# An attention and MLP kernel on one core: 25 words of its hand-written order of steps change places

## The chip, the core and the metric

The kernel runs on one core of a Trainium2 chip. The metric is device time in microseconds (us) of one execution, median over runs. The core has five engines with instruction queues of their own: PE (TensorE, the matmuls), DVE (VectorE), ACT (ScalarE), POOL (GpSimd) and SP (SyncE, which here only issues DMAs). DMAs issued by SP go through one queue (q1 in the profile, "hardware dynamic"), those issued by POOL through another (q0, "software dynamic"). Both queues are served by the same 16 DMA engines.

## The reference

```python
scores = scale * q @ k.T                      # 8 batches x 8 heads, 576 positions, 64 wide
cum = cumsum(maximum(s, 0))
bias = -(cum[:, None] - cum[None, :])
scores = where(causal, -1e9, scores + minimum(bias, 0))
attn = softmax(scores)
x = concat_heads(attn @ v)                    # 8 x 576 x 512
xn = (x - mean(x)) / sqrt(var(x) + 1e-6) * g_ln
out = x + relu(xn @ w_ch1) @ w_ch2            # 512 -> 2048 -> 512
```

## The kernel before

The work is one list of steps, `PLAN` (from L1318), written out by hand. A loop at its end calls each word's function in that order; every function issues instructions to one or more engines, and each engine then runs its own instructions strictly in that order. Nothing reorders them later, so an instruction that waits holds back all that stands behind it on its engine, and a DMA that waits on SP holds back every later DMA of SP.

There are three phases. Batch 0 is done tile by tile (128 positions at a time, tile 4 being the last 64): `T.t.g` transposes, `S.t.g.i` scores, `x` exponentials, `V.t.g` times v, `N` normalises, `B`, `A` and `L.t` take the LayerNorm statistics and apply them, `X.t` transposes the result for the MLP. Batch 1 goes head by head: `s.n` scores of head n (8 to 15), `d.n` the scores of its last 64 positions, `v.n` times v, `n.n` normalisation. Batches 2 to 7 go by pairs of heads: `B2.n` the scores of pair n, `bx` exponentials (ACT), `bm` causal masks (POOL), `Y.n.i` times v (PE), `K.n.i` normalisation (DVE). The MLP of each batch is cut into units that the words `u` and `U` take one by one from a queue and that fill PE between the attention steps: 512-wide matmuls of the first product (`ph`, L792) and of the second (`py`, L811); in batch 0 part of the first product is cut by tiles (`piece`, L1087).

Data come in two ways:

- POOL's queue, float32 to bfloat16 on the way: `w1.c` and `w2.i` are quarters of the two MLP weights (512 KB of bfloat16 each, L253 and L256), `lp.g` is `kp` and `qp` of pair g (L184; pairs 4 to 7 are batch 1's, 8 to 11 batch 2's), `LV.b.t` a tile of v (L192). POOL gives its DMAs eight completion semaphores in turn, so a DMA is issued only when the one eight places ahead of it has landed.
- SP's queue, float32: `lr.b.t` loads one tile of k and one of q of batch b (L206, `rowtmp`, 256 KB each), `lv.b.t` one tile of v. POOL casts k and q (`cr`, L218) and weights v (`vm`, L233); `tr` transposes by DMA (L225). `aug` (the words `aug` and `a3`, L265 and L267) copies rows of the gate sums beside q and k; `a3` writes into `kq[1]`, which batch 0's scores of heads 4 to 7 read, so it waits for the last of these.

`Q.q.g` and `Q.k.g` are the transposes of pair g on PE (`trqk`, L323), which read `qp` and `kp`; `E` copies them out of PSUM. `W.n` is n dummy matmuls (`idle`, L889). `Sk` are the scores of batch 0's last 64 keys (L1014). `fv.0` clears a part of `v_bf` (POOL). `Da.b.4` is a DMA transpose on SP (L759), `la.b.t` LayerNorm of tile t of batch b (DVE).

Of the kernel before, what the change touches and what calls it, by code (L numbers as in the profile page):

```python
# [16 lines left out]
P = 128  # L17
# [13 lines left out]
def fast_path(  # L31
# [13 lines left out]
    B, H, S, D = q.shape  # L45
# [13 lines left out]
    G = 4  # L59
# [896 lines left out]
    E = {"A": "act", "D": "dve", "P": "pool", "S": "sync"}  # L956
# [249 lines left out]
    def raise_flag(count, ones, n):  # L1206
# [120 lines left out]
        S.3.0.2 B.0.1 T.3.1 B.1.0 x.2.1.0 e.3.1:D B.1.1 S.3.0.0 S.3.0.3 y.0:A aug x.3.0.2 V.2.0 M.0.0.0 x.3.0.3
        M.0.0.3 S.3.0.1 V.2.1 S.3.1.1 x.3.0.1 N.2.0 M.0.0.2 bc.4 S.3.1.3 x.3.0.0 X.1 x.3.1.3 y.1:A N.2.1 M.0.0.1
        S.3.1.2 V.3.0 S.3.1.0 M.0.1.3 L.2 T.4.0 M.0.1.0 r.0.0:A N.3.0 X.2 x.3.1.2 Q.q.4 x.3.1.0 x.3.1.1 e.4.0:D
        T.4.1 y.2:D M.0.1.2 Q.k.4 E.q.4.0:A B.3.0 E.k.4.0:A S.4.0.1 e.4.1:D S.4.1.0 M.0.1.1 E.q.4.1:D E.k.4.1:D  # L1330
        x.4.0.1 x.4.1.0 U A.1 V.3.1 s.8 N.3.1 u L.3 B.2.1 B.2.0 d.8 S.4.0.0 X.3 y.3:A r.0.1:D Q.q.5 E.q.5.1:A
# [287 lines left out]
```

## Time and profile before

| | us |
|---|---|
| median of 3 runs | 344.21 (342.92 to 344.62) |
| the profiled execution | 346.36 |
| its span, first to last instruction | 344.9 |
| PE busy in the span | 331.5 |
| DVE, ACT, POOL busy | 199.5, 187.7, 168.6 |

The profiled execution is 2.15 us (0.6%) above the median of the runs; its span is 1.46 us shorter than its time. Times of the views are microseconds from the start of the span. A timeline row gives start, duration, engine, line, operation, output and input, count, and in brackets how long the engine sat idle before it and what released it. A windows row gives the window and its length, then busy time and instructions of PE, PEld, DVE, ACT and POOL, the clock granted to PE as a share, the mean busy share of the DMA engines (over 1 where packets overlap), and GB/s.

### The profile page before, as it was taken

The page shows a single profiled execution, that of the slowest core. Times are in us where ns is not written, and L with a number is a line of the kernel's source. Part 1 is how long each engine was busy: PE and PEld are TensorE (multiplying, and loading weights), DVE is VectorE, ACT ScalarE, POOL GpSimd, SP SyncE. Part 2 cuts the span into 40 slices and gives each one's busy share as a digit, 9 for nine tenths or more (in the row PEclk, how much of TensorE's full clock was granted, in tenths as well). Part 3 has the DMA queues.
Part 4 walks back from the last instruction along what each step waited for, and adds up shares of the span by engine and source line. Part 5 has one row for each costly group of instructions (what it writes and reads, how often), then busy time and mean ns, then how long its engine had stood idle before and what let it go on. Part 6 is the DMA issues. An engine that isn't in the chain of part 4 may idle for free.

```text
span 344.9 us, 8061 instructions
## 1 busy us (share of the span) xinstructions
PE 331.5 (96%) x3117; PEld 183.3 (53%) x3117; DVE 199.5 (58%) x567; ACT 187.7 (54%) x348; POOL 168.6 (49%) x305
## 2 busy tenths in 40 slices
PE   6999989989998998999999999999999999999993
PEld 2899756545554554555555545554455444444443
DVE  6598777837685675347653664566448624523421
ACT  4998899677664675357736774486344204202200
POOL 8896768777377947683984377441301001000000
PEclk9899999999999999999999999999999999999998
DMA  9999999999999999999998966700510141020022
GB/s 144 181 189 177 172 193 195 214 208 233 164 215 227 169 245 195 216 228 198 205 209 205 214 108 151 139 2 2 121 63 2 24 129 46 3 90 33 2 62 65
DMA packets 147962, 48.59 MB, mean 141 GB/s; under 512 B 135280, under 2 KB 143760, under 8 KB 147920
## 3 DMA queue, kind: packets, MB, share of 16 engines
q1 hardware_dynamic: 121856, 38.34, 57.3%
q0 software_dynamic: 24304, 8.92, 22.0%
q10 hardware_dynamic: 1760, 0.79, 0.9%
q8 instruction: 25, 0.41, 0.5%
q14 instruction: 17, 0.14, 0.1%
HBM read 37.11 MB, written 9.44 MB: 135 GB/s over the span
## 4 chain that ended last, share of the span: by engine, by line
PE 77%; DMA 10%; POOL 7%; DVE 1%; issue 1%; SPq 1%; ACT 0%; POOLq 0%; DVEq 0%
PE py L811 34%; PE ph L792 31%; DMA v_bf<-in_v_dram 5%; PE pot L626 4%; DMA kp<-in_k_dram 3%; PE sa L553 2%; DMA rowtmp<-in_k_dram 2%; PE sb L553 1%; PE sc L553 1%; PE pott L664 1%; DMA rowtmp<-in_v_dram 1%; POOL rowb L180 1%; PE pot L590 1%; SPq L206 1%; POOL v_bf L233 1%
## 5 line engine op out<-in xcount | busy, mean ns | idle before, releaser
L811 PE MATMUL py<-w_bf,hT 128*128 128x512 bf16 (+2 forms) x608 | 131.1, 368 | 0.1
L792 PE MATMUL ph<-xT,w_bf 128*128 128x512 bf16 x480 | 109.8, 379 | 0.2 <-ACT er L560 0.2
L783 ACT ACTIVATE hT<-ph 128x512 bf16<-128x512 f32 x102 | 60.9, 604 | 77.6 <-PE ph L792 76.1
L811 PEld LDWEIGHTS <-hT 128*128 128x128 bf16 x608 | 55.9, 98 | 59.8
L792 PEld LDWEIGHTS <-w_bf 128*128 128x128 bf16 x544 | 51.3, 98 | 56.5 <-issue 0.3
L497 POOL TENSOR_SCALAR_AFFINE_SELECT er<-er 128x256 bf16<-128x256 bf16 x96 | 38.8, 419 | 48.7 <-ACT er L560 34.3
L823 DVE SCALAR_TENSOR_TENSOR yo<-py,rstd,xb 128x512 f32<-128x512 f32 x32 | 24.0, 751 | 50.5 <-PE py L811 46.2
L560 ACT ACTIVATE er<-sb 128x512 bf16<-128x512 f32 x48 | 28.2, 609 | 22.1 <-PE sb L553 17.9
L781 DVE TENSOR_SCALAR hT<-ph 128x512 bf16<-128x512 f32 x34 | 23.5, 691 | 27.5 <-PE ph L792 26.0
L233 POOL TENSOR_TENSOR v_bf<-rowtmp,wt 128x512 bf16<-128x512 f32 (+1 forms) x30 | 33.1, 1107 | 10.0 <-DMA rowtmp<-in_v_dram 9.8
L560 ACT ACTIVATE er<-sa 128x512 bf16<-128x512 f32 x48 | 28.6, 609 | 16.4 <-PE sa L553 15.1
L560 ACT ACTIVATE er<-sc 128x512 bf16<-128x512 f32 x48 | 28.8, 614 | 3.8 <-PE sc L553 3.8
L626 PEld LDWEIGHTS <-er 128*128 128x128 bf16 x480 | 19.8, 97 | 12.8 <-POOL er L497 4.0
L715 POOL TENSOR_TENSOR rstd<-rstd,mhalf 128x4 f32<-128x4 f32 (+1 forms) x8 | 8.7, 1093 | 34.3 <-DVE rstd L714 34.2
L626 PE MATMUL pot<-v_bf,er 128*128 128x66 bf16 x480 | 22.5, 193 | 3.1 <-POOL er L497 2.1
L700 DVE BATCH_NORM_STATS2 stats<-xb 128x6 f32<-128x128 f32 (+1 forms) x84 | 24.8, 326 | 0.6
L741 DVE SCALAR_TENSOR_TENSOR xn<-xb,mv,gb 128x512 bf16<-128x512 f32 x28 | 24.5, 874 | 1.0
L218 POOL CAST kq<-rowtmp 128x512 bf16<-128x512 f32 (+1 forms) x30 | 19.0, 645 | 12.2 <-DMA rowtmp<-in_k_dram 11.8
L643 DVE TENSOR_REDUCE sums<-pot 128x4 f32<-128x8 f32 x48 | 7.8, 163 | 29.5 <-PE pot L626 29.1
L645 DVE TENSOR_TENSOR xb<-pot,rinvs 128x256 f32<-128x256 f32 x48 | 20.4, 424 | 1.7
L553 PEld LDWEIGHTS <-kq 64*128 64x128 bf16 x384 | 11.9, 94 | 9.6 <-issue 4.2
L218 POOL CAST rowb<-rowtmp 128x512 bf16<-128x512 f32 (+1 forms) x20 | 12.8, 652 | 3.3 <-DMA rowtmp<-in_k_dram 2.9
(178 smaller groups left out, 393.2 us busy)
## 6 DMA issues: line engine op xcount, KB each, us to landing
out_dram<-yo SPq DMA_DIRECT2D x32, 256.0 KB
rowtmp<-in_v_dram SPq DMA_DIRECT2D x24, 256.0 KB
rowtmp<-in_k_dram SPq DMA_DIRECT2D x20, 256.0 KB
rowtmp<-in_q_dram SPq DMA_DIRECT2D x20, 256.0 KB
w_bf<-in_moe_w_ch_dram POOLq DMA_DIRECT2D x8, 512.0 KB, 9.0
kp<-in_k_dram POOLq DMA_DIRECT2D x8, 144.0 KB, 10.2
qp<-in_q_dram POOLq DMA_DIRECT2D x8, 144.0 KB, 10.2
v_bf<-in_v_dram POOLq DMA_DIRECT2D x8, 128.0 KB, 8.3
```

The lines of the kernel that those rows point to most:

```text
L218: nc.gpsimd.tensor_copy(out=rows[b % 2][0:pn, t, u], in_=loaded.pop(("kq"[u], b, t))[0:pn])
L233: e.tensor_tensor(out=v_bf[b % 2][0:pn, t, :, 0:D], in0=loaded.pop(("v", b, t))[0:pn], in1=wt[0:pn, t, b, :].unsqueeze(2).to_broadcast([pn ...
L497: nc.gpsimd.affine_select(out=out, in_=out, compare_op=ALU.is_ge, fill=0.0, base=0, pattern=pattern, channel_multiplier=-1,)
L553: nc.tensor.matmul(a, lhsT=lhsT, rhs=rhs, start=True, stop=True)
L560: nc.scalar.activation(out=er[:, 2 * n % 4 + i, o : o + 512], in_=bank["B", n].pop((name, i)), func=ACT.Exp, scale=scale,)
L626: nc.tensor.matmul(pot[:, t, :], lhsT=e[:, o : o + P], rhs=v_bf[b % 2][:, kb, h, :], start=(kb == 0), stop=(kb == t),)
L700: nc.vector.bn_stats(out=st[b][:, t, part, :], in_=x_tiles(b)[t][:, lo:hi])
L741: nc.vector.scalar_tensor_tensor(out=xn, in0=tiles[t], scalar=mvs[b][:, t, 0:1] if b > 0 else mean0[:, t : t + 1], in1=gb, op0=ALU.subtrac ...
L783: nc.scalar.activation(out=dst, in_=ph, func=ACT.Relu)
L792: nc.tensor.matmul(ph, lhsT=w1_bf[:, kd, fb * P : (fb + 1) * P], rhs=xT[:, :, kd, :], start=(kd == 0), stop=(kd == KD - 1),)
L811: nc.tensor.matmul(py[t], lhsT=hT[:, fb, t * P : (t + 1) * P], rhs=w2_bf[:, fb, c0:c1], start=(fb == 0), stop=(fb == FB - 1),)
L823: nc.vector.scalar_tensor_tensor(out=yo, in0=py[t], scalar=rs, in1=x[:, c0:c1], op0=ALU.mult, op1=ALU.add)
```

## The change

The words stay the same 1305; 25 of them stand elsewhere. The table's rows tell little, so only two lines of its diff are shown:

```diff
-        lc.k.3 lc.q.3 g LV.0.2 w1.0 LV.0.3 lp.4 cr2.0 cr2.1 fv.1 fk.0 fk.1 lc.k.4 lc.q.4 w1.1 f.7 f.8 fv.0 lp.5
-        w1.2 f.9 f.10 LV.1.0 LV.1.1 LV.1.2 LV.1.3 LV.1.4 lp.6 LV.0.4 w1.3 w2.0 lp.7 lp.8 w2.1 f.11 relu.0 scan.0
+        lc.k.3 lc.q.3 g LV.0.2 w1.0 LV.0.3 lp.4 cr2.0 cr2.1 fv.1 fk.0 fk.1 lc.k.4 lc.q.4 w1.1 f.7 f.8 w1.2 fv.0
+        lp.5 f.9 f.10 LV.1.0 LV.1.1 LV.1.2 LV.1.3 LV.1.4 lp.6 LV.0.4 w1.3 w2.0 lp.7 lp.8 w2.1 f.11 relu.0 scan.0
...
```

By words:

- `w1.2` goes ahead of `fv.0` and `lp.5`.
- `W.1` (one dummy matmul) goes from between `T.0.0` and `hi.2` to just behind `scan.0`, so that it joins the nine at the start.
- `L.1` goes behind the two steps `B.0.1` and `B.1.0`.
- Around the end of batch 0: `S.4.1.1` goes ahead of `S.4.0.0`; `Q.q.5` and `Sk` ahead of `r.0.1`; `d.8` and `Q.k.5` behind the next `u wr u`; `B.0.0` and a `U` ahead of `v.8`.
- `a3` goes from ahead of `lr.3.1` to behind `N.4.1`, so on SP `lr.3.1` now stands ahead of it.
- Later: `K.9.0` ahead of `vm.3.0` and the LayerNorm of batch 1's last tile; `Da.1.4` and `bx.16.4` some ten words later; `la.3.1`, `lv.5.4`, `cr.6.3.0`, `cr.6.4.0`, `cr.6.1.0` and `Y.20.1` later.

On SP, near its start, the two loads of `lr.3.1` (`rowtmp`, k and q) and the four copies of `a3` into `kq_110` change places:

```order
 L265 DMA kq_111<-c_122 1x4x576
 L267 DMA kq_111<-c_122 1x4x576 x3
+L206 DMA rowtmp<-in_k_dram 128x8x64
+L206 DMA rowtmp<-in_q_dram 128x8x64
 L265 DMA kq_110<-c_122 1x4x576
 L267 DMA kq_110<-c_122 1x4x576 x3
-L206 DMA rowtmp<-in_k_dram 128x8x64
-L206 DMA rowtmp<-in_q_dram 128x8x64
 L206 DMA rowtmp<-in_v_dram 128x8x64
 L206 DMA rowtmp<-in_k_dram 128x8x64
```

The two loads have moved ahead of four copies that wait for PE; the loads themselves wait only for DMAs of the first microseconds, and their staging tiles are fresh. Everything behind keeps its order.

On POOL, between its early memsets, `w1.2` (`w_bf`) and the pair `lp.5` (`kp`, `qp`) change places:

```order
 L934 MEMSET v_bf_108 128x32
 L935 MEMSET v_bf_108 64x8
+L253 DMA w_bf<-in_moe_w_ch_dram 128x4x512
 L1314 MEMSET v_bf_107 64x528
 L184 DMA kp<-in_k_dram 96x2x384
 L184 DMA qp<-in_q_dram 96x2x384
-L253 DMA w_bf<-in_moe_w_ch_dram 128x4x512
 L937 MEMSET kq_111 128x8x64
 L192 DMA v_bf_108<-in_v_dram 128x8x64 x4
```

The weight quarter is now issued one memset and two loads sooner, and `kp` and `qp` of pair 5 stand behind it in the queue.

More of the change, by code (lines that the diff above doesn't have):

```diff
@@ L1327, in fast_path @@
[L1327 to L1331, printed above, removed]
@@ L1392, in fast_path @@
[L1392 to L1396 removed]
+        S.2.1.1 N.1.1 S.2.0.0 L.0 V.1.0 x.2.0.1 x.2.0.2 x.2.1.2 X.0 e.3.0:D N.1.0 x.2.1.1 x.2.0.0 S.2.1.0
@@ new lines, in fast_path @@
+        S.3.0.2 B.0.1 T.3.1 B.1.0 x.2.1.0 L.1 e.3.1:D B.1.1 S.3.0.0 S.3.0.3 y.0:A aug x.3.0.2 V.2.0 M.0.0.0
+        x.3.0.3 M.0.0.3 S.3.0.1 V.2.1 S.3.1.1 x.3.0.1 N.2.0 M.0.0.2 bc.4 S.3.1.3 x.3.0.0 X.1 x.3.1.3 y.1:A N.2.1
+        M.0.0.1 S.3.1.2 V.3.0 S.3.1.0 M.0.1.3 L.2 T.4.0 M.0.1.0 r.0.0:A N.3.0 X.2 x.3.1.2 Q.q.4 x.3.1.0 x.3.1.1
+        e.4.0:D T.4.1 y.2:D M.0.1.2 Q.k.4 E.q.4.0:A B.3.0 E.k.4.0:A S.4.0.1 e.4.1:D S.4.1.0 M.0.1.1 E.q.4.1:D
+        E.k.4.1:D x.4.0.1 x.4.1.0 U A.1 V.3.1 s.8 N.3.1 u L.3 B.2.1 B.2.0 S.4.1.1 S.4.0.0 X.3 y.3:A Q.q.5 Sk
@@ new lines, in fast_path @@
+        r.0.1:D E.q.5.1:A E.q.5.0:D x.4.1.1 x.4.0.0 u wr u d.8 Q.k.5 u B.0.0 U v.8 La.3 E.k.5.0:D B.3.1 n.8 xk
+        cr.3.0.0 lr.3.1 Q.k.6 E.k.6.0:A E.k.5.1:A u s.9 V.4.1 E.k.6.1:D N.4.1 a3 M.0.2.3 M.0.2.2 V.4.0 Q.q.6
+        N.4.0 s.10 v.9 A.3 qu.3 M.0.2.0 lp.11 d.10 A.2 M.0.2.1 E.q.6.0:D s.11 n.9 u Q.k.7 E.q.6.1:D w2.2 d.12
+        s.12 r.0.2:A E.k.7.0:D E.k.7.1:D O2.k.8:A v.10 n.10 Q.q.7 u s.13 E.q.7.0:D w2.3 E.q.7.1:D wT v.11 lp.10
+        u wx n.11 ga.1.0.2 lv.2.0 A.0 u d.14 ga.1.0.0 v.12 qu.4 n.12 O2.k.9:A s.14 cr.3.1.0 ga.1.0.3 u F.k.8
@@ new lines, in fast_path @@
+        v.13 u R qu.5 n.13 La.6 F.k.9 ga.1.1.2 s.15 v.14 u G.k.9:D ga.1.1.0 n.14 U v.15 O2.q.8:A O2.q.9:A U n.15
+        F.q.9 qu.6 lr.3.2 O2.k.11:A vo.2:P u ga.1.2.0 ga.1.2.1 ga.1.0.1 La.2 me cr.3.1.1 u l.0 O2.q.11:A F.q.8 U
+        ga.1.1.3 ga.1.1.1 lv.2.1 l.1 lv.2.2 G.k.8:A ga.1.2.2 vm.2.0:P vo.3:P ga.1.2.3 lr.3.3 F.k.11 lv.2.3 u l.3
+        F.q.11 cr.3.0.1 lv.2.4 l.2 G.q.11:D G.q.8:A G.q.9:A cr.3.2.0 G.k.11:A O2.k.10:A D lr.3.4 u U F.k.10 U
+        O2.q.10:A G.k.10:A F.q.10 to G.q.10:A u lv.3.0 U lr.4.0 tk.2 vm.2.1:P B2.8 vm.2.2:P bx.8.3 u bx.8.1
@@ new lines, in fast_path @@
+        vm.2.3:P sd.2 bx.8.4 vm.2.4:P bx.8.2 qu.7 se.2 u bx.8.5 sm.2 ga.1.0.4 u bx.8.0 bm.8.3 u bm.8.1 B2.9
+        bm.8.2 bm.8.0 bx.9.5 Y.8.1 ga.1.1.4 lr.4.1 cr.3.2.1 bx.9.4 cr.3.3.0 bx.9.0 Y.8.0 cr.3.3.1 K.8.0 tr.3.0.2
+        bm.9.3 cr.3.4.1 K.8.1 bx.9.2 bm.9.0 bx.9.3 bx.9.1 bm.9.1 u bm.9.2 U u u Y.9.0 K.9.0 vm.3.0:P ga.1.2.4
+        la.1.4 B2.10 bx.10.0 bx.10.3 bx.10.4 bx.10.2 bx.10.5 cr.3.4.0 bm.10.3 bx.10.1 Y.9.1 U K.9.1 u tr.3.2.4 u
+        U u lv.3.1 tr.3.4.5 bm.10.1 Y.10.1 bm.10.0 B2.11 bx.11.0 bx.11.4 lv.3.2 bx.11.5 lv.3.3 K.10.1 bm.10.2
@@ new lines, in fast_path @@
+        Y.10.0 K.10.0 bm.11.2 ga.2.0.0 lv.3.4 bx.11.2 bm.11.0 La.4 bx.11.1 u ga.2.1.2 ga.2.0.3 U u cr.4.1.1
+        lr.4.2 bx.11.3 Y.11.0 K.11.0 bm.11.3 u U bm.11.1 u ga.2.0.1 lr.4.3 cr.4.0.1 vm.3.1:P Y.11.1 K.11.1
+        lv.4.0 lv.4.1 tk.3 vm.3.4:P lr.4.4 u ga.2.1.0 u Z.2 z.2 B2.12 bx.12.0 vm.3.2:P U bx.12.4 bm.12.2
+        ga.2.1.1 bx.12.1 lv.4.2 ga.2.2.0 cr.4.2.1 ga.2.2.1 ga.2.1.3 lv.4.3 la.2.0 la.2.1 cr.4.0.0 bx.12.5
+        bm.12.3 vm.3.3:P cr.4.1.0 ga.2.2.2 bx.12.3 bm.12.1 u bx.12.2 bm.12.0 u u sd.3 se.3 u B2.13 bx.13.5
@@ new lines, in fast_path @@
+        bx.13.1 ga.2.0.2 la.2.2 u bx.13.0 cr.4.4.0 sm.3 u bx.13.4 ga.2.2.3 u la.2.3 Da.2.0 bx.13.3 u Y.12.0
+        bx.13.2 bm.13.0 K.12.0 u u B2.14 cr.4.4.1 tr.4.4.5 bx.14.2 Y.12.1 K.12.1 bx.14.1 bm.13.2 bx.14.3 vo.4:P
+        bx.14.4 u u u tr.4.0.2 bx.14.5 bm.13.1 bm.13.3 bx.14.0 Y.13.0 B2.15 bx.15.0 K.13.0 bx.15.2 cr.4.3.1
+        cr.4.2.0 cr.4.3.0 tr.4.2.4 u lr.5.0 u vm.4.1:P Y.13.1 bx.15.3 bx.15.5 bx.15.1 u K.13.1 bx.15.4 bm.14.1
+        bm.14.2 bm.15.0 tk.4 ga.3.0.0 U U bm.14.0 u bm.15.1 Y.14.0 K.14.0 bm.14.3 Y.14.1 K.14.1 sd.4 ga.3.1.1
@@ new lines, in fast_path @@
+        ga.3.1.3 ga.3.1.0 se.4 u vm.4.0:P u u lv.4.4 bm.15.3 lv.5.0 Y.15.1 ga.3.0.1 K.15.1 vm.4.3:P Z.3 z.3
+        B2.16 bx.16.0 bx.16.2 vm.4.2:P bm.15.2 Y.15.0 K.15.0 sm.4 vm.4.4:P bx.16.3 bx.16.1 bm.16.1 bx.16.5
+        bm.16.3 u ga.3.2.3 U bm.16.0 lr.5.1 cr.5.1.0 ga.3.1.2 cr.5.0.0 u Da.1.4 bx.16.4 u ga.3.0.3 lv.5.2
+        ga.3.0.2 u u bm.16.2 u Y.16.0 ga.3.2.1 cr.5.1.1 ga.3.2.0 lr.5.3 cr.5.3.0 B2.17 bx.17.0 bx.17.1 la.3.0
+        vm.5.2:P K.16.0 bx.17.4 lr.5.4 lr.6.0 lv.5.3 Y.16.1 lr.5.2 K.16.1 bm.17.2 lv.5.1 ga.3.2.2 cr.5.4.0 u
@@ new lines, in fast_path @@
+        cr.5.4.1 bx.17.2 bx.17.3 bm.17.0 la.3.2 la.3.3 cr.5.2.0 bm.17.1 tr.5.4.5 bx.17.5 bm.17.3 lr.6.1 u la.3.1
+        u qm u u cr.5.3.1 u cr.5.2.1 u tk.5 vo.5:P cr.6.1.1 Da.3.0 u lv.6.0 u Y.17.0 B2.18 bx.18.3 bx.18.2
+        bx.18.0 K.17.0 bx.18.1 u u Y.17.1 K.17.1 bx.18.4 bx.18.5 bm.18.3 tr.5.2.4 u u ga.3.1.4 ga.3.0.4 B2.19
+        bx.19.0 vm.5.3:P bx.19.3 bm.18.2 ga.4.0.1 bm.18.1 cr.5.0.1 bm.18.0 tr.5.0.2 vm.5.0:P bx.19.1 u bm.19.1 u
+        u lv.6.1 sd.5 u bx.19.5 lv.5.4 se.5 Y.18.1 sm.5 K.18.1 u vm.5.1:P Y.18.0 ga.3.2.4 la.3.4 bx.19.2 U u u U
@@ new lines, in fast_path @@
+        ga.4.0.3 bm.19.3 bx.19.4 bm.19.2 u u ga.4.0.2 u K.18.0 ga.4.1.0 bm.19.0 Y.19.0 K.19.0 Z.4 z.4 B2.20
+        bx.20.0 vm.5.4:P ga.4.1.2 bx.20.2 lr.6.2 lr.6.3 Y.19.1 K.19.1 ga.4.2.2 bx.20.3 bx.20.4 bm.20.2 lv.6.2
+        bm.20.0 cr.6.2.0 ga.4.2.3 u ga.4.2.0 u vm.6.1:P bx.20.5 bm.20.3 cr.6.0.1 bx.20.1 u u u ga.4.1.1 bm.20.1
+        ga.4.0.0 Y.20.0 K.20.0 u u u u cr.6.3.1 lr.6.4 lr.7.0 lv.6.3 ga.4.2.1 vo.6:P B2.21 bx.21.4 bm.21.2
+        lr.7.1 la.4.0 la.4.1 u bx.21.1 ga.4.1.3 cr.6.3.0 cr.6.4.0 Y.20.1 K.20.1 la.4.2 bx.21.2 bx.21.0 cr.6.4.1
@@ new lines, in fast_path @@
+        bm.21.0 cr.6.1.0 cr.6.2.1 u u bx.21.3 u u tr.6.4.5 Y.21.0 bx.21.5 bm.21.3 B2.22 u bx.22.0 la.4.3 Da.4.0
+        bm.21.1 K.21.0 bx.22.4 cr.6.0.0 tr.6.0.2 bx.22.3 u u bx.22.5 bm.22.3 u Y.21.1 bx.22.2 La.7 K.21.1
+        cr.7.1.0 bx.22.1 bm.22.2 tk.6 u u vm.6.3:P tr.6.2.4 B2.23 bx.23.2 bx.23.4 bx.23.0 bx.23.3 bm.22.0
+        bm.22.1 bx.23.1 u u u vm.6.0:P bx.23.5 bm.23.0 u sd.6 se.6 u u Y.22.1 u cr.7.0.1 K.22.1 ga.5.0.0 Y.22.0
+        K.22.0 ga.5.0.1 u u bm.23.3 lr.7.2 u vm.6.2:P cr.7.1.1 bm.23.1 Y.23.1 K.23.1 bm.23.2 Z.5 z.5 B2.24
@@ new lines, in fast_path @@
+        bx.24.0 Y.23.0 ga.5.0.3 K.23.0 lr.7.3 lv.6.4 bx.24.3 ga.5.1.4 ga.5.2.4 cr.7.3.0 lv.7.0 sm.6 ga.5.1.3
+        bx.24.4 bm.24.2 ga.5.2.0 u lv.7.1 La.5 ga.5.2.1 u u bx.24.2 bm.24.0 ga.5.1.1 U vm.6.4:P ga.5.1.0 la.5.0
+        bx.24.5 bx.24.1 bm.24.3 vm.7.0:P ga.5.0.4 lv.7.2 u bm.24.1 lv.7.3 ga.5.2.2 u u Y.24.0 K.24.0 Da.3.4 u u
+        lr.7.4 cr.7.4.0 u ga.5.2.3 u cr.7.0.0 tr.7.0.2 cr.7.4.1 tr.7.4.5 lv.7.4 B2.25 bx.25.2 bx.25.4 vo.7:P
+        bx.25.0 bx.25.5 bx.25.1 bx.25.3 bm.25.2 la.5.1 Y.24.1 u K.24.1 ga.5.0.2 u ga.5.1.2 la.5.2 u la.5.3
@@ new lines, in fast_path @@
+        Da.5.0 cr.7.3.1 bm.25.1 u u u u cr.7.2.0 B2.26 bx.26.3 bm.25.0 vm.7.2:P bx.26.4 Y.25.0 bx.26.2 K.25.0
+        cr.7.2.1 bx.26.1 bm.26.2 u u u bm.25.3 Y.25.1 bx.26.0 bx.26.5 K.25.1 ga.6.0.0 vm.7.3:P bm.26.0 B2.27
+        bx.27.0 u tk.7 bx.27.4 sd.7 bx.27.3 bm.27.2 bx.27.5 u ga.6.0.3 u bm.26.3 bm.26.1 se.7 la.5.4 tr.7.2.4 u
+        u U Y.26.1 u U sm.7 bx.27.1 bm.27.1 Da.5.4 Y.26.0 K.26.0 bm.27.3 K.26.1 ga.6.1.2 bx.27.2 bm.27.0
+        vm.7.4:P ga.6.1.3 u vm.7.1:P u u Y.27.0 K.27.0 ga.6.1.0 Z.6 z.6 B2.28 bx.28.0 ga.6.0.2 bx.28.1 bx.28.3
@@ new lines, in fast_path @@
+        bx.28.4 Y.27.1 bm.28.2 bx.28.2 bm.28.0 u u ga.6.1.1 bx.28.5 u u K.27.1 ga.6.2.2 u bm.28.3 Y.28.0
+        ga.6.2.0 K.28.0 u u la.6.0 bm.28.1 Y.28.1 u u u u B2.29 bx.29.1 bx.29.2 ga.6.2.3 K.28.1 ga.6.0.1 u
+        bx.29.4 bm.29.2 bx.29.3 ga.6.2.1 la.6.1 la.6.2 la.6.3 u u u bm.29.1 u u u bx.29.0 bx.29.5 bm.29.0 Y.29.0
+        B2.30 bx.30.0 bx.30.5 K.29.0 u u bm.29.3 Y.29.1 K.29.1 ga.7.0.2 bx.30.4 bx.30.2 Da.6.0 u bm.30.2 u
+        bx.30.3 bm.30.0 bx.30.1 B2.31 bx.31.3 u u ga.7.0.1 u u bx.31.0 bx.31.5 bx.31.2 ga.7.0.3 Y.30.0 K.30.0 u
@@ new lines, in fast_path @@
+        bm.30.1 U u U bm.30.3 bx.31.1 bm.31.1 Y.30.1 K.30.1 ga.7.1.0 bm.31.3 ga.7.1.3 bx.31.4 bm.31.2 u U Y.31.1
+        K.31.1 U bm.31.0 ga.7.1.2 u Y.31.0 K.31.0 u Z.7 z.7 ga.7.2.2 ga.7.2.3 ga.7.2.0 u ga.7.0.4 ga.7.1.4
+        ga.7.2.4 ga.7.1.1 u u u U ga.7.0.0 u u u u la.7.0 ga.7.2.1 la.7.1 la.7.2 la.7.3 Da.7.0 u u u u u u u u u
+        u u u u u u u u U u U u la.7.4 U u U u u u u U U gd u Da.7.4 u u u u u u u u u u u u u u u u U u u u U U
+        U u u U u U U U U fl u u u u u u vl u u u u u u u u u u u u u u u u u u
```

70 lines of the change are left out of this document (2 added, 68 removed).

## The prediction

> **What bounds the kernel now.** I read the page first, then windows, PE's timeline at its waits, the chain, and last the two DMA queues. The page:
>
> ```profile
> span 344.9 us, 8061 instructions
> PEclk9899999999999999999999999999999999999998
> DMA  9999999999999999999998966700510141020022
> ```
>
> The DMA engines are busy in the first 21 of 40 slices, to about 181 us, and PE's clock dips in the first slices only. Then five windows, of which the last is the rest of the span from 131 us on:
>
> ```profile
> 24.00:28.00 4.00, 4.00 (x89) 3.93 (x86) 3.75 (x10) 4.00 (x9) 4.00 (x6) 1.00 1.25 192
> 36.00:40.00 4.00, 4.00 (x53) 2.73 (x53) 3.01 (x7) 3.30 (x7) 3.18 (x6) 1.00 1.20 185
> 46.00:50.00 4.00, 4.00 (x56) 2.70 (x54) 3.83 (x8) 4.00 (x9) 3.00 (x8) 1.00 1.22 193
> 64.00:68.00 4.00, 4.00 (x30) 2.08 (x29) 3.93 (x7) 2.45 (x4) 2.28 (x5) 1.00 0.89 196
> 131.00:345.00 214.00, 207.81 (x1610) 104.21 (x1610) 107.70 (x304) 89.43 (x165) 70.62 (x131) 0.99 0.53 108
> ```
>
> From 131 us on PE is busy 207.8 of 214 us, the rest being the end of the span. So the part behind 131 us keeps its length, and the change can act only through what happens before. Behind the first 15 us of that PE waits at five places:
>
> ```profile
> 31.39 0.41 PE L323 MATMUL trqk<-ident,qp 96*128 96x96 bf16 x6 [0.20 <-ACT er L438]
> 45.11 0.43 PE L323 MATMUL trqk<-ident,kp 96*128 96x96 bf16 x6 [0.98 <-DMA kp<-in_k_dram]
> 74.94 0.48 PE L626 MATMUL pot<-v_bf,er 128*128 128x66 bf16 x10 [0.75 <-POOL er L497]
> 75.65 0.48 PE L626 MATMUL pot<-v_bf,er 128*128 128x66 bf16 x10 [0.24 <-POOL er L497]
> 105.96 0.48 PE L626 MATMUL pot<-v_bf,er 128*128 128x66 bf16 x10 [1.00 <-DVE rstd L714]
> 131.63 0.33 PE L626 MATMUL pot<-v_bf,er 128*128 128x66 bf16 x5 [1.13 <-POOL er L497]
> ```
>
> The chain says what stands behind three of them:
>
> ```profile
> 35.09 9.98 DMA kp<-in_k_dram
> 45.11 0.43 PE trqk L323 x6
> ...
> 69.03 3.42 DMA rowtmp<-in_v_dram
> 72.51 1.03 POOL v_bf L233
> 74.16 1.44 POOL er L497 x4
> 75.65 0.48 PE pot L626 x10
> ...
> 124.66 5.34 DMA rowtmp<-in_k_dram
> 130.05 1.16 POOL kq L218 x2
> 131.22 0.37 POOL er L497
> 131.63 0.33 PE pot L626 x5
> ```
>
> At 45.11 PE waits for `kp` of pair 7 (`Q.k.7`) from POOL's DMA queue; at 75 and 131 us for POOL, which waits for rows of SP's queue. All three are DMA waits. The one at 105.96 is a loop between PE and DVE and moves with PE.
>
> **The change part by part.** The term that counts is `a3`, which changes places with `lr.3.1`. SP before:
>
> ```profile
> 18.27 1.95 SPq L267 DMA_DIRECT2D kq<-c  x3
> 32.85 0.57 SPq L265 DMA_DIRECT2D kq<-c  x1
> 33.48 1.81 SPq L267 DMA_DIRECT2D kq<-c  x3
> 35.33 0.47 SPq L206 DMA_DIRECT2D rowtmp<-in_k_dram  x1
> 35.84 0.82 SPq L206 DMA_DIRECT2D rowtmp<-in_q_dram  x1
> 36.70 6.54 SPq L206 DMA_DIRECT2D rowtmp<-in_v_dram  x1
> 43.29 4.41 SPq L206 DMA_DIRECT2D rowtmp<-in_k_dram  x1
> 66.07 0.53 SPq L206 DMA_DIRECT2D rowtmp<-in_q_dram  x1
> ```
>
> SP stood idle from 20.2 to 32.85 (`a3` waited for PE), and all of SP's loads stood behind it. With the change `lr.3.1` is issued at 20.2, 15 us sooner; `a3` still goes at about 33, and `lv.2.0`, which came third at 36.7, follows at about 35.3. So SP's queue moves two loads of 256 KB that it did not move in this stretch, and from 36 on it has work as before. The DMA engines have no room for them: in 24 to 28 us they have only POOL's loads and are at a busy share of 1.25, with 192 GB/s, the same as in 46 to 50 us, where SP's loads run between POOL's (1.22, 193 GB/s). A load of SP's thus takes its time from POOL's: SP's third and fourth load held it for 6.54 and 4.41 us beside POOL's loads, against 0.53 us at 66.07 without. The price is the time of 2 x 262 KB at the 196 GB/s of 64 to 68 us, where SP has the engines alone: 524/196 = 2.7 us. Bounds: 0, if the pieces slip between POOL's; 3.2 us, if SP's following loads too start a little sooner and take a further half us. I take 2.7, since the equal GB/s of the two windows speaks for a full trade.
>
> Every load of POOL's issued from then on lands up to 2.7 us later: `kp` of pair 7 at 47.8 instead of 45.1. `Q.k.7` is not moved, and PE starts it at 47.8: **2.7 us late**.
>
> `w1.2` ahead of `lp.5`. POOL's rows:
>
> ```profile
> 22.54 0.64 POOL L184 DMA_DIRECT2D qp<-in_q_dram  x1
> 23.16 0.79 POOL L253 DMA_DIRECT2D w_bf<-in_moe_w_ch_dram  x1
> 30.84 0.70 POOL L192 DMA_DIRECT2D v_bf<-in_v_dram  x1 [0.89 <-DMA w_bf<-in_moe_w_ch_dram]
> ```
>
> The DMA at 30.84 waited for `w1.2`, so these three loads were through at 30.8. In the new order `qp` of pair 5 is last of them and lands at 30.8 by itself, and some 1.4 us later with half of `lr.3.1` between (0 to 2.7): at 32.2. PE wants it (`Q.q.5`) at 31.2, where the wait on ACT of 0.20 us goes, because `d.8` no longer holds a PSUM tile just ahead. So PE waits there 1.0 us (0 to 2.3) instead of 0.2. This is covered: PE reached `Q.k.7` at 44.13 before and reaches it at about 44.9 now, while `kp` comes at 47.8. Without that cover it would cost 0.8. The wait at `Q.k.7` itself becomes 2.9 us.
>
> What is covered in the same way, since it all lies ahead of 45 us where PE waits anyway: `W.1` (its matmul goes to a stretch in which PE waits for DVE), `L.1` (0.75 us later on DVE, its transposes 2 us away), `d.8`, `S.4.1.1`, `Sk`, `Q.k.5`, `B.0.0` and `U` (the same work in another order). The steps behind 80 us add nothing to PE, which waits neither before nor behind them, but at 105.96 for DVE and at 131.63 for POOL: `K.9.0` frees a PSUM tile 2 us sooner that nobody waits for; the others move single DMAs, casts and one `Y` by less than PE's queue of MLP units covers. I put them at 0, between -0.2 and +0.3 us.
>
> From 47.8 on PE, ACT and POOL run 2.7 us late, in step with POOL's loads, which stay 2.7 us late to their end. Then the DMA engines come even: as many bytes have been moved as before, only SP's loads sooner and POOL's later. So the load of v that lands at 72.45 lands there again, and POOL's masks are ready at 75.65. PE arrived at 74.19 (74.94 less 0.75) and now arrives at 76.9; the 0.75 and 0.24 us of waiting go, and 2.7 - 0.99 = 1.7 us are left. The wait at 105.96 moves with PE. At 131.63 the load of k again lands by the DMA engines' count, the wait of 1.13 us goes, and 1.7 - 1.13 = **0.6 us** are left, which PE carries to the end. Against the profiled execution's 346.36 that is 347.0; against the median, 344.21 + 0.6 = **344.8 us**.
>
> The clock could add to this. The windows at the start:
>
> ```profile
> 4.38:7.79 3.41, 1.72 (x8) 0.45 (x6) 2.81 (x12) 2.16 (x5) 3.33 (x6) 1.00 1.54 175
> 7.79:11.20 3.41, 3.26 (x29) 3.01 (x30) 1.88 (x8) 2.48 (x4) 3.35 (x5) 0.50 1.92 175
> ```
>
> After a stretch of 3.4 us in which PE was busy 1.72 us, half of it, its clock was halved for the next 3.4 us. Waits of 1.0 and 1.1 us (at 45, 75, 105 and 131 us) did not bring that. A wait of 2.9 us, mostly within one such stretch, would leave PE less than half busy. The Trainium skill, "TensorE: Matmul & The Clock Gate", section "What's actually happening", has the clock halved only after a window of about 3.4 us that is idle; by that sentence a wait of 2.9 us costs nothing more and the sum stays 344.8. By the row it costs half of 3.4 us, 1.7, and the sum would be 346.5. The row shows it once, at the start, behind an idle time; I keep the sum without it and make it a rival.
>
> **The rivals.**
>
> 1. Slower: the clock. Place: the 3.4 us behind the wait at `Q.k.7`; price 1.7 us of PE's time on top, all waits behind being used up, so 0.6 + 1.7 = 2.3 and **346.5**. It decides once more than about 1.7 us of the wait (half a stretch, as in the row at 4.38) falls into one stretch. For it: the half-busy stretch at the start. Against: the page's PEclk shows no other dip, and part of the wait may fall into each of two stretches. Chance 0.25.
> 2. Slower: nothing is given back. SP's loads of 65 to 131 us wait for buffers that POOL frees behind PE; if these waits bind, being late at 47.8 makes the loads late, and the waits at 75 and 131 us stay. Then 1.7 to 2.7 us stay, **346.4** in the middle. For it: in 62 to 76 us POOL stands behind ACT and PE. Against: SP's loads took longer than issue alone in this stretch, so the DMA engines, not POOL, set their pace. Chance 0.12.
> 3. Faster: the two loads fit between POOL's pieces at no cost. Then `kp` lands as before, SP's queue is 2.7 us ahead, and the waits at 75 and 131 us go: 0.99 + 1.13 = 2.1, **342.1**. For it: SP's queue was idle for 12 us. Against: busy shares over 1 and equal GB/s. Chance 0.10.
> 4. The loads don't go sooner at all, because something else holds them on SP: **344.2**. Their only waits are DMAs of the first microseconds; chance 0.03.
>
> **How the numbers follow.** The forecast, 344.8, has the remaining 0.50; its own range, with 1.5 to 3.2 us at `Q.k.7` and the later steps' -0.2 to +0.3, is 344.0 to 345.6. A measurement of this kernel can tell about 0.5%, 1.7 us, from no change. Slower by more: most of rival 1 (0.18), over half of rival 2 (0.08), 0.02 of the forecast: 0.28. Faster by more: most of rival 3 and a little for what I overlook: 0.10. The same: 0.62. The range takes in the forecast and most of rivals 1 and 2, and leaves out rival 3 and the ends of 1 and 2: 343.3 to 346.9.
>
> **What the profile after would show.** On SP the loads of `lr.3.1` at 20.2 instead of 35.3, and `a3` at about 33. On PE a wait at the `qp` of pair 5 of about 1 us, and at the `kp` of pair 7 one of 2.9 us that ends at 47.8. No wait, or a short one, at 75 and at 131 us. A clock of 1.00 in 46 to 54 us; 0.50 there would be rival 1. I am wrong in the main term if `kp` of pair 7 lands at 46 or sooner, and in the giving back if PE still waits 1 us at both later places.

## The result, and the profile after

After takes 345.99 us in the median of 13 runs (344.35 to 348.45), before 343.91 in 13 runs beside it (342.63 to 345.76): a ratio of 1.0059, 95% interval 1.0034 to 1.0083. The change costs 2.08 us, where 0.6 were forecast. The 345.99 lies in the range put on record (343.3 to 346.9), but above the range of the forecast itself (344.0 to 345.6).

SP's timeline after (start, duration, operation):

```profile
20.38 0.43 SPq L206 DMA_DIRECT2D rowtmp<-in_k_dram  x1
20.87 0.74 SPq L206 DMA_DIRECT2D rowtmp<-in_q_dram  x1
34.14 0.58 SPq L265 DMA_DIRECT2D kq<-c  x1
36.62 0.44 SPq L206 DMA_DIRECT2D rowtmp<-in_v_dram  x1
```

The two loads of `lr.3.1` are issued at 20.4 instead of 35.3 us, `a3` follows at 34.1. PE's timeline after, at `Q.q.5`, at `Q.k.7` and at its end:

```profile
33.04 0.43 PE L323 MATMUL trqk<-ident,qp 96*128 96x96 bf16 x6 [1.71 <-DMA qp<-in_q_dram]
...
47.35 0.43 PE L323 MATMUL trqk<-ident,kp 96*128 96x96 bf16 x6
...
338.32 0.16 PE L1406 MATMUL after<-mark,hT 128*128 128x1 bf16 x1 [0.47 <-DVE mark L1404]
```

`Q.k.7` starts at 47.35 instead of 45.11, 2.24 us late. It shows no wait, but the chain has the load right before it:

```profile
37.01 10.30 DMA kp<-in_k_dram
47.35 0.43 PE trqk L323 x6
```

PE came there just as `kp` landed, because it had lost time before. It waited 1.71 us at `Q.q.5`, and the windows (length, then busy time of PE, PEld, DVE, ACT, POOL, PE's clock, DMA share, GB/s) show what came of that:

```profile
30.22:33.64 3.42, 1.71 (x45) 1.54 (x43) 1.80 (x4) 1.79 (x5) 1.64 (x3) 1.00 1.80 164
33.64:37.05 3.41, 3.41 (x41) 3.41 (x38) 2.10 (x5) 2.35 (x4) 1.87 (x4) 0.50 2.05 168
37.05:40.46 3.41, 3.41 (x58) 2.73 (x57) 0.92 (x2) 2.04 (x5) 2.78 (x5) 1.00 1.34 183
```

The stretch with the wait has PE busy for half of it, and the clock is halved in the next one. That is the forecast's rival 1, at another place. The wait of 2.9 us that was forecast at `Q.k.7` is not there: PE spent that time before it.

Behind 47 us PE doesn't wait for longer than 0.2 us up to 337 us. The waits of before at 75, 106 and 131 us (3.1 us in all) are gone, and by these two profiled executions after ends *sooner* than before: its last matmul is at 338.32 instead of 339.92, its time 344.71 instead of 346.36. The medians say the opposite. The profiled execution of before was longer than any of its 13 timed runs, that of after one of the shortest of its 13. So the first question to the chip was which of these waits belong to the kernel.

### The profile page after: what moved, and what is told of

Its sections match the earlier page's. It is cut to its first block, busy times and chain, and to the rows that moved or that the text cites. A ratio compares the mean times of both kernels' runs of the same rounds, so it can differ in the third digit from the quotient of the medians.

```text
span 343.2 us, 8064 instructions
## 1 busy us (share of the span) xinstructions
PE 332.4 (97%) x3117; PEld 183.6 (54%) x3117; DVE 197.4 (58%) x567; ACT 187.5 (55%) x348; POOL 168.0 (49%) x305
## 2 busy tenths in 40 slices
DMA packets 147962, 48.59 MB, mean 142 GB/s; under 512 B 135280, under 2 KB 143760, under 8 KB 147920
## 4 chain that ended last, share of the span: by engine, by line
PE 84%; DMA 8%; POOL 5%; issue 1%; DVE 0%; POOLq 0%
PE py L811 37%; PE ph L792 34%; DMA v_bf<-in_v_dram 5%; PE pot L626 5%; DMA kp<-in_k_dram 3%; PE sa L553 2%; PE sc L553 1%; PE sb L553 1%; PE pott L664 1%; POOL rowb L180 1%; PE pot L590 1%; PE trp L361 1%; POOL w_bf L253 1%; POOL kq L951 1%; POOL v_bf L192 1%
## 5 line engine op out<-in xcount | busy, mean ns | idle before, releaser
L233 POOL TENSOR_TENSOR v_bf<-rowtmp,wt 128x512 bf16<-128x512 f32 (+1 forms) x30 | 32.3, 1086 | 8.2 <-DMA rowtmp<-in_v_dram 8.0
L741 DVE SCALAR_TENSOR_TENSOR xn<-xb,mv,gb 128x512 bf16<-128x512 f32 x28 | 23.3, 833 | 1.0
L645 DVE TENSOR_TENSOR xb<-pot,rinvs 128x256 f32<-128x256 f32 x48 | 20.4, 424 | 1.7
L792 PE MATMUL ph<-xTm,w_bf 128*128 128x512 bf16 x64 | 14.0, 379 | 0.0
```

Of the source, the lines that this page charges most:

```text
L233: e.tensor_tensor(out=v_bf[b % 2][0:pn, t, :, 0:D], in0=loaded.pop(("v", b, t))[0:pn], in1=wt[0:pn, t, b, :].unsqueeze(2).to_broadcast([pn ...
L741: nc.vector.scalar_tensor_tensor(out=xn, in0=tiles[t], scalar=mvs[b][:, t, 0:1] if b > 0 else mean0[:, t : t + 1], in1=gb, op0=ALU.subtrac ...
L792: nc.tensor.matmul(ph, lhsT=w1_bf[:, kd, fb * P : (fb + 1) * P], rhs=xT[:, :, kd, :], start=(kd == 0), stop=(kd == KD - 1),)
```

## The experiments

Each is an edit of the list of steps. Ratios are to runs of before on the same chip, with their 95% interval.

**1. Both kernels once more.** No edit.

> The kernel before, once more, for a second profiled execution. The theory (waits of one execution were taken for the rule): the time is 1.000 of before within 0.002; kp of pair 7 again ends a wait of about 1.0 us of PE at 45.1 us, and the waits at 75 us again come to about 1 us, but those at 105.96 (1.00 us, DVE) and 131.63 (1.13 us, POOL) are much shorter, together under 0.7 us, if the profiled execution is near the median of 343.9 us instead of 346.4. The rival (the waits are there in every execution, and the change's cost lies elsewhere): both are there again with about 1 us each.

> The kernel after, once more. Ratio again 1.004 to 1.008. PE waits for qp of pair 5 at about 32 us for 1.5 to 2 us; the clock is halved in the following stretch only if the stretch that holds the wait has PE busy for less than about 2.05 of 3.41 us (the bound that eight profiles so far show: halved behind 1.65 to 2.03, not behind 2.07 and more). If it isn't halved, PE reaches Q.k.7 earlier and waits there until kp of pair 7 lands at 47.3 us: the lateness behind is the same. Rival, clock: without the halved clock the lateness behind Q.k.7 and the time are 1.7 us less.

Before: 0.9999 (0.9977 to 1.0020); its profiled execution took 342.87 us. After: 1.0057 (1.0027 to 1.0088), 346.73 us in the profile. PE's waits in the second profile of before:

```profile
44.78 0.43 PE L323 MATMUL trqk<-ident,kp 96*128 96x96 bf16 x6 [0.23 <-DMA kp<-in_k_dram]
...
74.21 0.47 PE L626 MATMUL pot<-v_bf,er 128*128 128x66 bf16 x10 [0.36 <-POOL er L497]
74.92 0.48 PE L626 MATMUL pot<-v_bf,er 128*128 128x66 bf16 x10 [0.24 <-POOL er L497]
...
336.71 0.16 PE L1406 MATMUL after<-mark,hT 128*128 128x1 bf16 x1 [0.47 <-DVE mark L1404]
```

and in that of after:

```profile
33.11 0.43 PE L323 MATMUL trqk<-ident,qp 96*128 96x96 bf16 x6 [1.67 <-DMA qp<-in_q_dram]
...
48.40 0.43 PE L323 MATMUL trqk<-ident,kp 96*128 96x96 bf16 x6 [1.03 <-DMA kp<-in_k_dram]
...
106.34 1.89 PE L811 MATMUL py<-w_bf,hT 128*128 128x512 bf16 x8 [0.92 <-DVE yo L823]
...
340.76 0.16 PE L1406 MATMUL after<-mark,hT 128*128 128x1 bf16 x1 [0.47 <-DVE mark L1404]
```

The waits of before at 45 and 74 us are there again, smaller; those at 106 and 131 us are not. After has a wait of 0.92 us at 106 in one execution and none in the other. The halved clock behind `Q.q.5` came both times.

**2. The swap on SP alone, and after without it.**

```diff
 (a3_only: before)
- cr.3.0.0 a3 lr.3.1 Q.k.6
+ cr.3.0.0 lr.3.1 a3 Q.k.6
 (after_a3_back: after)
- cr.3.0.0 lr.3.1 Q.k.6 E.k.6.0:A E.k.5.1:A u s.9 V.4.1 E.k.6.1:D N.4.1 a3
+ cr.3.0.0 Q.k.6 E.k.6.0:A E.k.5.1:A u s.9 V.4.1 E.k.6.1:D N.4.1 a3 lr.3.1
```

> Before, with a3 and lr.3.1 alone changing places on SP. The theory (the two loads of 256 KB trade one to one with POOL's, and little of it is given back): kp of pair 7 lands at about 47.3 us instead of 45.1, the wait of PE at Q.k.7 is about 3.2 us, and the time is 1.5 to 2.2 us over before, ratio 1.0045 to 1.0065. Rival, clock: as the wait at Q.k.7 is more than half of 3.4 us, a halved clock follows it and the time is 3 to 4 us over before, ratio 1.009 to 1.012. Rival, other moves: the swap alone costs nothing at the end, ratio 1.000, though kp lands later.

> After, with lr.3.1 put back behind a3 on SP. The theory: kp of pair 7 lands at 45 us again and the time is that of before, ratio 0.999 to 1.001. Rival, other moves: it stays at 1.005 to 1.007. Rival, clock: if the wait at Q.q.5 still has more than 1.7 us and halves the clock, PE arrives late at Q.k.7 and about 1 us stays, ratio 1.003; by the theory this wait is shorter, as half of lr.3.1 no longer lies ahead of qp of pair 5.

The swap alone: 1.0053 (1.0032 to 1.0073). After without it: 1.0009 (0.9991 to 1.0027). So the swap carries the change's cost, and all the other moves together, in the order without the swap, nothing that can be measured. (The shortest list of moved words that turns before into after has 20, those named under "The change", not 25.) PE with the swap alone:

```profile
36.60 0.28 PE L590 MATMUL pot<-v_bf,er 128*128 128x65 bf16 x4 [0.74 <-DMA v_bf<-in_v_dram]
37.50 0.64 PE L590 MATMUL pot<-v_bf,er 128*128 128x65 bf16 x6 [0.62 <-DMA v_bf<-in_v_dram]
...
47.25 0.43 PE L323 MATMUL trqk<-ident,kp 96*128 96x96 bf16 x6 [1.07 <-DMA kp<-in_k_dram]
...
338.48 0.16 PE L1406 MATMUL after<-mark,hT 128*128 128x1 bf16 x1 [0.47 <-DVE mark L1404]
```

Against the second profile of before, which like this one has no wait of over 0.2 us behind 75 us, `Q.k.7` is 47.25 - 44.78 = 2.47 us late and the end 338.48 - 336.71 = 1.77: the 0.36 and 0.24 us of waiting at 74 us are given back, and almost nothing else. The wait at `Q.k.7` was 1.07 us, not 3.2 as expected: the loads of v for batch 1's first head (`v.8`) land late too, and PE already loses 1.36 us to them at 36 us.

**3. A third load ahead of `a3`.**

```diff
- cr.3.0.0 a3 lr.3.1 Q.k.6
+ cr.3.0.0 lr.3.1 lv.2.0 a3 Q.k.6
  (and lv.2.0 is taken from its old place)
```

> Before, with three loads of 256 KB (lr.3.1 and lv.2.0) ahead of a3 on SP instead of two. The theory (each byte of SP's that goes sooner takes its time from POOL's loads): kp of pair 7 lands 262/196 = 1.3 us later than with two, at about 48.5 us, and the time is about 1.3 us over that run, ratio to before 1.008 to 1.010. Rival, saturation: the third load goes at the cost of nothing more, kp stays at 47.2 and the ratio at 1.005. Rival, given back: kp at 48.5, but later waits of PE take the difference, ratio 1.005 to 1.006.

1.0152 (1.0132 to 1.0172): 3.4 us more than with two loads, not 1.3. PE and SP in it:

```profile
37.40 0.25 PE L590 MATMUL pot<-v_bf,er 128*128 128x65 bf16 x3 [1.14 <-DMA v_bf<-in_v_dram]
...
50.12 0.43 PE L323 MATMUL trqk<-ident,kp 96*128 96x96 bf16 x6 [0.50 <-DMA kp<-in_k_dram]
```

```profile
21.66 5.00 SPq L206 DMA_DIRECT2D rowtmp<-in_v_dram  x1
32.60 0.58 SPq L265 DMA_DIRECT2D kq<-c  x1
...
35.08 0.44 SPq L206 DMA_DIRECT2D rowtmp<-in_k_dram  x1
35.56 0.58 SPq L206 DMA_DIRECT2D rowtmp<-in_q_dram  x1
36.19 11.39 SPq L206 DMA_DIRECT2D rowtmp<-in_v_dram  x2
```

The expected rivals, that the third load costs nothing more or that later waits take it up, are both out. `Q.k.7` is another 2.9 us late, about what two loads were priced at. The load of `kp` with two loads ahead and with three:

```profile
36.84 10.37 DMA kp<-in_k_dram
38.38 11.70 DMA kp<-in_k_dram
```

It is issued 1.54 us later and then takes 1.33 us longer. The second part fits SP's queue, which is a load ahead as a whole: behind `a3`, at 35 us, it issues k and q of the next tile and two loads of v, where with two loads ahead (and in after, at 36.62) a load of v came first. So the likely reading is that a step moved ahead on a queue is paid with the loads that move up behind it as well; no run holds these later loads back to show it. This run also has a halved clock from 40.06 us on (last section), which the wait for `kp` covers.

**4. `w1.2`, alone and put back.**

```diff
 (w12_only: before)
- f.7 f.8 fv.0 lp.5 w1.2
+ f.7 f.8 w1.2 fv.0 lp.5
 (after_w12_back and w12_back_again: after, the same the other way round)
```

> Before, with w1.2 alone moved ahead of lp.5. The theory (its place is covered): kp of pair 7 lands at about 45 us as in before, qp of pair 5 lands at about 30.8 us by the time PE wants it, and the time is that of before, ratio 0.998 to 1.002. Rival, w1.2: what after gains over the run with w1.2 put back, 1.2 us, is a gain of this move by itself, and the ratio is 0.996 to 0.997.

> After, with w1.2 behind lp.5 again. kp of pair 7 lands at 47.3 us as in after, since the same loads go ahead of it. The theory: the wait of 1.71 us at Q.q.5 goes or shrinks below 0.7 us, no halved clock follows there, PE is some 2 us earlier at Q.k.7 and waits there for as much longer (about 2 us instead of 0.06), and the time stays that of after, ratio 1.005 to 1.007. Rival, clock: the halved clock behind Q.q.5 is what the change costs, and the ratio falls to 1.000 to 1.002.

> After with w1.2 behind lp.5 again, beside after on one chip. If the difference of 1.2 us to after was that of w1.2, it is there again: ratio about 1.010 and over that of after by 0.003 or more. Rival, chance: PE waited 0.94 us at 104.8 us behind one xn of DVE of 4.35 us, which is not part of every execution; then the ratio is within 0.002 of after's.

Alone: 1.0008 (0.9983 to 1.0032), nothing. Put back: 1.0100 (1.0079 to 1.0122), and beside the second run of after 1.0103 (1.0044 to 1.0162) against its 1.0057. So it is not that the late wait at `Q.q.5` costs: without it the kernel is slower by 0.004, twice (the intervals overlap, a little in the first pair and much in the second). Nor do the parts add up: with `w1.2` at its old place the swap alone is at 1.0053, and the swap with the other moves at 1.0100, the intervals apart. So these moves, worth nothing without the swap, cost some 0.005 with it, and `w1.2` takes most of that back. The profile of the repeat shows one way in which that comes about, PE's timeline and the windows:

```profile
48.59 0.43 PE L323 MATMUL trqk<-ident,kp 96*128 96x96 bf16 x6 [2.43 <-DMA kp<-in_k_dram]
```

```profile
46.87:50.28 3.41, 1.69 (x31) 1.36 (x32) 1.21 (x2) 1.25 (x4) 1.81 (x4) 1.00 1.26 191
50.28:53.70 3.42, 3.42 (x17) 1.38 (x14) 2.90 (x6) 3.04 (x7) 2.21 (x6) 0.50 1.22 194
```

Here PE came to `Q.k.7` early and waited there, half of a stretch was idle, and the clock was halved behind `Q.k.7`, where no wait is left to cover it. Against the profile of after, `Q.k.7` is 48.59 - 47.35 = 1.24 us later, and the last matmul, at 341.19, 2.87 us: 1.63 more. (Against the second profile of after it is 0.24 more, but that one has a wait of 0.92 us behind, which this one has not.) This is rival 1 at its own place and near its price. The first profile with `w1.2` put back has no halved clock there. It loses its time at another place:

```profile
99.19 4.35 DVE L741 SCALAR_TENSOR_TENSOR xn<-xb,mv,gb 128x512 bf16<-128x512 f32 x1
```

```profile
105.75 1.89 PE L811 MATMUL py<-w_bf,hT 128*128 128x512 bf16 x8 [0.94 <-DVE yo L823]
```

Its `Q.k.7`, at 47.78, is 0.43 us later than in the profile of after, its last matmul, at 340.18, 1.86: 1.43 more, of which 0.94 are this wait behind a long instruction on DVE (last section). These are two executions with two reasons; how often each comes in the timed runs, and so what the 0.004 is made of, stays open.

**5. `kp` of pair 7 taken out of the way.**

```diff
 (after_lp7: after; before_lp7: before; a3_lp7: a3_only)
- w1.3 w2.0 lp.7 lp.8
+ w1.3 lp.7 w2.0 lp.8
 (lp7_lv: before_lp7, and)
- lr.3.3 F.k.11 lv.2.3 u l.3 F.q.11 cr.3.0.1 lv.2.4
+ F.k.11 lv.2.3 u l.3 F.q.11 cr.3.0.1 lv.2.4 lr.3.3
```

> After, with the loads of pair 7 ahead of w2.0 on POOL. kp of pair 7 then lands at about 44 us, before PE wants it. The theory (two things hold PE in after, each enough alone: the late kp of pair 7, and the wait at Q.q.5 with the halved clock behind it): where the clock is halved PE still reaches Q.k.7 at 47.3 us and nothing is gained, where it isn't PE gains up to 1.7 us there, ratio to before 1.002 to 1.005. Rival, one cause: kp of pair 7 alone holds PE, the ratio falls to 1.000. Rival, later loads: as all of POOL's loads stay 2.3 us late, another one is waited for, ratio 1.006.

> Before, with a3 and lr.3.1 changing places, and the loads of pair 7 ahead of w2.0 on POOL. The theory (the swap makes each of POOL's loads late, and PE uses them as they land): kp of pair 7 lands at about 44 us and the wait at Q.k.7 goes (1.07 us), but the waits for v_bf at 36 us stay (1.4 us), so 1.0 us of the 1.8 us of the swap are won back and the ratio is 1.002 to 1.0035. Rival, one load: kp of pair 7 alone carries the swap's cost, ratio 1.000. Rival, later loads: w2.0 or the pairs behind are waited for instead, ratio 1.005.

> Before, with the loads of pair 7 ahead of w2.0 on POOL and nothing else. The theory: the wait at Q.k.7 (0.2 to 1.0 us) goes, and up to that is won, ratio 0.998 to 0.9995, as PE then waits longer at 74 us for rows of v. Rival: a move of loads ahead of PE's wants costs something elsewhere, as the run with the third load of lr.3 moved did, ratio 1.001 to 1.003.

> Before, with two other moves, against the two waits that every execution shows: the loads of pair 7 go ahead of w2.0 on POOL, and the third load of rows of lr.3 goes behind the last of lv.2 on SP. The theory: kp of pair 7 lands at about 42 us, before PE wants it, the waits at 45 us (0.2 to 1.0) and at 74 us (0.6) go, and the time falls by 0.5 to 1.5 us, ratio 0.996 to 0.9985. Rival, taken elsewhere: other loads (w2.0, or lr.3.3 for the casts of batch 3) are waited for instead, ratio 1.000 or over.

None of the four gains, and the median of each came out slower than the theory had it; only for before_lp7, and at its edge for a3_lp7, does the interval reach what the theory had: after_lp7 1.0096 (1.0075 to 1.0117), a3_lp7 1.0055 (1.0032 to 1.0078), before_lp7 1.0005 (0.9978 to 1.0032), lp7_lv 1.0024 (1.0000 to 1.0047). The wait at `Q.k.7` went in all four. With the swap it is not this one load that holds PE. The windows of a3_lp7:

```profile
35.40:38.81 3.41, 1.25 (x23) 0.97 (x21) 0.52 (x2) 1.28 (x3) 1.68 (x4) 1.00 1.69 169
38.81:42.22 3.41, 3.27 (x14) 1.52 (x14) 2.04 (x6) 0.81 (x2) 3.31 (x6) 0.50 1.30 207
```

PE stands idle for 2.2 us of the first, waiting for v, and is halved in the second, and so starts `Q.k.7` at 48.5 without any wait. Without the swap (before_lp7) PE starts `Q.k.7` at 43.8, a microsecond or more sooner than in before, but waits behind 100 us:

```profile
104.35 0.48 PE L626 MATMUL pot<-v_bf,er 128*128 128x66 bf16 x10 [1.03 <-DVE rstd L714]
...
130.38 0.33 PE L626 MATMUL pot<-v_bf,er 128*128 128x66 bf16 x5 [1.15 <-POOL er L497]
```

The first profile of before has such waits too, and against that one before_lp7 ends 1.24 us sooner (338.68), against the second, without them, 1.97 us later. Of the gain at `Q.k.7` the medians show nothing; why is open. Why after_lp7 is rather slower than after (the intervals hardly overlap) is not settled. No version was measurably faster than before.

## Where the forecast held, and the step that failed

**`a3` and `lr.3.1`: right.** The loads went at 20.4, as forecast; `Q.k.7`, forecast for 47.8, came at 47.35 and 48.40 in the two profiles of after, and at 47.25 with the swap alone. Forecast 2.7 us late; against the mean of before's two profiles (44.95) it is 2.4 and 3.5. The path there was another one: PE was to stand at `Q.k.7` from 44.9 on and wait 2.9 us, and it came there late itself. Rivals 3 and 4 (the loads fit in free, or don't go sooner) are out. The third load shows the trade from the other side.

**`w1.2` and the wait at `Q.q.5`: covered, but larger than forecast.** The wait was 1.7 us, inside the bounds of 0 to 2.3, and it brought a halved clock. Both were covered by `kp` of pair 7, as the step said. What the step didn't see is that in the order without this move PE can run into a longer wait at `Q.k.7` (2.43 us in one of two profiles, 1.04 in the other).

**The other words at 0: right without the swap**, 1.0009. With the swap they are not at 0 one by one (experiment 4).

**Giving back: here the forecast failed.** The step took 0.75 and 0.24 us at 75 us and 1.13 us at 131 us as won back, and left 0.6 of 2.7. The first part holds: both profiles of after and that of the swap alone have no wait at 75 us. The second doesn't. It read "At 131.63 the load of k again lands by the DMA engines' count, the wait of 1.13 us goes", from one execution, and took the wait of 1.00 us at 105.96 for a loop of PE and DVE that moves with PE. In the second profile of before both waits are missing. By the sign that the prediction gave (wrong if PE still waits 1 us at both places) this step would have held, since after does not wait there; but a wait that before has only in some executions can't be counted in full. What differs is a stretch at 92 us in the first, the windows of before:

```profile
92.00:94.00 2.00, 2.00 (x19) 1.08 (x18) 1.59 (x6) 0.97 (x2) 0.00 (x0) 1.00 1.66 47
```

and of its second execution:

```profile
92.00:94.00 2.00, 1.95 (x29) 0.93 (x28) 0.97 (x4) 0.93 (x2) 0.79 (x2) 1.00 0.91 201
```

For two microseconds the DMA engines move a quarter of what they otherwise move, with a busy share of 1.66. SP's loads behind it are late. POOL's timeline in the first:

```profile
98.30 2.56 POOL L233 TENSOR_TENSOR v_bf<-rowtmp,wt 64x512 bf16<-64x512 f32 x2 [2.14 <-DMA rowtmp<-in_v_dram]
...
130.05 1.16 POOL L218 CAST kq<-rowtmp 128x512 bf16<-128x512 f32 x2 [2.32 <-DMA rowtmp<-in_k_dram]
```

and the same two steps in the second:

```profile
95.91 2.03 POOL L233 TENSOR_TENSOR v_bf<-rowtmp,wt 64x512 bf16<-64x512 f32 x2 [2.27 <-DMA rowtmp<-in_v_dram]
...
125.40 1.17 POOL L218 CAST kq<-rowtmp 128x512 bf16<-128x512 f32 x2 [0.42 <-DMA rowtmp<-in_k_dram]
```

They are 2.4 and 4.7 us apart, PE only 0.7 and 1.9 us. Of the six profiles with `lr.3.1` at its old place four have this stretch between 90 and 93 us, with 45 to 76 GB/s, and these four are the ones with waits at 104 and 130 us; of the eight with it sooner none has it there. That these waits come from this stretch is argued from this, not shown: no run brings it about or takes it away, and why the swap should keep it off, if it does, is open.

So the sum with what both kernels show in each profile is: about 2.9 us late at `Q.k.7` (47.88 less 44.95, means of two), less 0.8 at 75 us (mean of 0.99 and 0.60), 2.1. The medians give 2.08. That these agree so closely is in part luck. Behind 100 us before waited 2.13 us in one execution and not in the other, after not in the one and 0.92 in the other; with the means of these the sum would be 1.5, and the last matmuls of the two profiles of each are 1.2 us apart in the mean. How often the timed runs have these waits is not on record. So the step that failed is the 1.13 us booked in full at 131 us, from one execution; what the waits behind 100 us are worth on average stays open.

That the measured time lies in the range is not owed to the sum either: the range reaches so far up because of rivals 1 and 2.

**Rival 2** (nothing given back, 346.4) comes nearest to the measured 345.99, but not by its mechanism: SP's loads did not keep the wait at 75 us alive. **Rival 1** (the clock) is real: the halved clock came behind `Q.q.5`, covered, and in one run behind `Q.k.7`, where PE lost up to 1.63 us, about its price of 1.7.

## What to carry to other kernels

Before a wait far behind the edit is booked as slack that will take up a delay, look whether it is in a second execution; the one profile at hand was 0.7% (2.45 us) above the median, and two of its waits, 2.13 us, are missing in its second execution. A load moved ahead on one DMA queue was paid here by the other queue, and what stood behind it on its own queue moved up too. Moves that cost nothing by themselves can cost something together with another. And where a wait must be, let it stand where another wait behind it covers a halved clock.

## What the runs showed of the hardware

**The clock is halved behind a stretch in which PE is idle for more than about 1.4 of 3.41 us.** Over the 14 profiles, stretches at full clock with PE busy for 1.06 to 1.90 us were all followed by a halved one, and those with 2.07 and more by none; of the two between, 2.01 was not (the repeat with `w1.2` put back, 36.63 us) and 2.02 was (after without the swap, 5.32 us). One halved stretch, in after_lp7 at 7.79 us with PE busy for 3.07, was followed by a second one. The least busy one, in the kernel with three loads:

```profile
36.65:40.06 3.41, 1.06 (x14) 0.68 (x14) 0.00 (x0) 0.00 (x0) 2.42 (x4) 1.00 1.64 193
40.06:43.48 3.42, 3.42 (x14) 1.54 (x13) 2.59 (x6) 1.36 (x2) 2.70 (x5) 0.50 1.30 210
```

and one above the bound, with the swap alone:

```profile
34.01:37.42 3.41, 2.12 (x40) 1.93 (x38) 1.70 (x4) 2.22 (x4) 2.09 (x3) 1.00 1.90 171
37.42:40.84 3.42, 3.20 (x29) 1.89 (x29) 2.54 (x6) 1.52 (x2) 3.06 (x7) 1.00 1.33 198
```

The stretches lie on a grid of 3.41 us that is shifted from one execution to the next (the halved one behind `Q.q.5` begins at 33.64 in one profile of after and at 34.73 in the other), so the same wait may halve the clock in one and not in another. The Trainium skill, "TensorE: Matmul & The Clock Gate", section "What's actually happening", lets the clock fall after a window of some 3.4 us that is idle, and calls the window free-running. The free-running grid agrees with the traces; the idle window doesn't, since 1.7 us of waiting in one were enough.

**One LayerNorm instruction on DVE took 4.33 us instead of 0.75.** In four of the 14 profiles one instruction of this line took 3.2 to 4.4 us. DVE's timeline in the second profile of after:

```profile
99.80 4.33 DVE L741 SCALAR_TENSOR_TENSOR xn<-xb,mv,gb 128x512 bf16<-128x512 f32 x1
```

POOL worked from 98.14 to 104.75 us without a break there, and the wait of PE at 106.34 follows. In the first profile of after the same instruction took 0.75 us beside a busy POOL, and it was POOL whose two casts took longer:

```profile
98.91 2.08 POOL L218 CAST rowb<-rowtmp 128x512 bf16<-128x512 f32 x2
```

against 1.16 us in the second. The Trainium skill, "SBUF — State Buffer", section "Who interferes with whom", has a DVE instruction with two inputs in SBUF (`xb` and `gb` here) contend with a POOL instruction that reads SBUF, for a pair of ports that is an exclusive lock, and the order of issue decide which of them waits. The two executions agree with that, one each way. That DVE took more than 4 us, over several of POOL's instructions, goes beyond it; that it was the lock all that time is not shown.
